# Transposing u by the DMA crossbar from SBUF to SBUF instead of by TensorE, with held x loads and zero fills on ScalarE, in a causal conv + low-rank mixer kernel

## The chip, the cores and the metric

One core of a Trainium2 chip. The metric is the device time of one execution in microseconds (us); the tables give the median of the executions. Engines are called as the profile calls them: PE is TensorE's matmul, PEld its weight load, DVE VectorE, ACT ScalarE, POOL GpSimd, SP SyncE, which only issues DMAs here; SPq is its queue.

## The reference

Inputs are float32, B = 8 batches, S = 4224 tokens, D = 192 channels in 8 heads of 24.

```python
w = softmax(weight)                                   # 8 heads x 7 taps
y[b, s, h, :] = sum_k w[h, k] * x[b, s - 6 + k, h, :] # causal conv, zeros before the start
h = (y^T @ U) @ V                                     # low rank 32, along the sequence
u = y + h^T
out = u + relu(u @ w_ch1) @ w_ch2                     # 192 -> 768 -> 192
```

(The names are shortened; the original computes the conv by unfolding and einsum.)

## The kernel before

Tokens are cut into 8 x 33 tiles of 128, and 8 tiles make a group, so there are 33 groups. For each group u must be turned around (channels onto partitions) before w1 can be multiplied. The kernel interleaves, in each iteration g: the w1 matmuls of group g, the w2 matmuls of group g-1, the conv of the next batch (when there is some left to do), `h_unit` (which makes u of group g+2) and the transposes of group g+1. Batch b+1's x is loaded into the buffer of batch b-1.

```python
def load_x(b):
    if b > 1:
        x_tiles[b], xh_tiles[b] = x_tiles[b - 2], xh_tiles[b - 2]
    nc.gpsimd.dma_start(out=x_tiles[b][:, 1 : 1 + NT, :], in_=x[b].rearrange(...))
    load_xh(b)
...
def tr_unit(g):
    def full():
        ps = [bank()[:].bitcast(BF16) for _ in range(2)]      # two PSUM banks
        uT = uTs.tile([P, 3, TOK], BF16, name="uT")
        for c in range(3):
            for i in range(Q):                                # 12 transposes of 128x128
                nc.tensor.transpose(out=ps[c // 2][...], in_=u_ring[:, r0 // 2 + i, c * P : (c + 1) * P],
                                    identity=ident[:])
        nc.vector.tensor_copy(out=uT[:, 0:2, :], in_=ps[0])
        nc.scalar.activation(out=uT[:, 2, :], in_=ps[1][:, 0:TOK], func=ACT.Copy)
    return None, full
...
for g in range(NG + 1):
    for k in range(2):
        if g < NG:
            for m in range(3):
                w1_piece(g, 3 * k + m, ...)       # 6 matmuls each, rhs = uT of group g
        units = side(2 * g + k)                   # conv heads, tt; after tt: load_x of the batch after
        if k and g + 2 < NG:
            units = [h_unit(g + 2, 0), h_unit(g + 2, 1)] + units
        ...
        run(*early)
        if g > 0:
            w2_piece(g - 1, k * 24, k * 24 + 12)  # also out = ch + u on DVE, and a store on SP
        run(*late)
        if k == 0 and g + 1 < NG:
            run(tr_unit(g + 1))
        if g > 0:
            w2_piece(g - 1, k * 24 + 12, k * 24 + 24)
```

The output tiles have 4 buffers, and each group makes 4 stores: DVE can run one group ahead of the stores, no more.

## Time and profile before

| | before |
|---|---|
| time, median of 4 executions | 410.61 us |
| span of the profiled execution | 407.7 us |
| PE busy | 92% |
| group without conv | 9.43 us |
| first w1 matmul at | 38.02 us |

The page of the kernel before, cut. Part 1 has busy time, share of the span and instruction count of each engine; part 3 the DMA queues with packets, MB, and the time of their packets as a share of 16 engines' span; part 4 the chain of work that ended last; part 6 the DMA issues with their count, size and median time from issue to landing.

```profile
PE 376.5 (92%) x3978; PEld 248.1 (61%) x3978; DVE 286.1 (70%) x514; ACT 218.0 (53%) x412; POOL 30.4 (7%) x34
...
q0 software_dynamic: 34960, 13.31, 28.1%
q1 hardware_dynamic: 40464, 30.04, 24.6%
...
PE 90%; ACT 4%; DVE 4%; DMA 1%; issue 1%; DVEq 0%
PE un L349 33%; PE ch L370 33%; PE un L255 7%; PE un L329 6%; PE un L244 5%; PE un L301 4%; PE un L275 2%; DVE U_sb L405 1%; DMA w_sb<-in_weight_dram 1%; DVE sm L160 1%; DVE u_ring L312 0%; ACT rl_476 L358 0%; DVE x_sb_162 L69 0%; ACT x_sb_
...
out_dram<-o SPq DMA_DIRECT2D x132, 192.0 KB, 2.0
```

PE is the bound: it is on 90% of the chain. The PE transposes (line 329) alone have 6% of it. Stores (the hardware queue, q1) and x loads (the software queue, q0) use the DMA engines about half the time.

The timeline of PE near the end, where no conv is left; columns are start and duration in us, then the instructions, merged into rows of one kind.

```profile
340.36 2.12 PE L349 MATMUL un<-uT,W_sb 64*128 64x512 bf16 x18
...
349.79 2.12 PE L349 MATMUL un<-uT,W_sb 64*128 64x512 bf16 x18
...
357.46 0.83 PE L329 MATMUL un<-ident,u_ring 128*128 128x128 bf16 x12
358.13 0.66 PE L370 MATMUL ch<-W_sb,rl_5345 128*128 128x192 bf16 x6
```

From one group's w1 start to the next is 349.79 - 340.36 = 9.43 us, with no gap. The 12 transposes start at 357.46 and the matmul after them at 358.13: they cost 0.67 us of PE's order (the duration shown, 0.83, includes the last one's drain, which overlaps).

The start of the kernel, timeline of all engines, cut to what the argument touches.

```profile
5.28 2.81 POOL L90 MEMSET xh_163<- 64x3264 f32 x1
...
5.56 2.56 DVE L160 TENSOR_SCALAR sm<-sm 128x8 f32<-128x8 f32 x1
8.15 0.20 DVE L162 RECIPROCAL rs<-sm 128x8 f32<-128x8 f32 x1
...
22.22 2.84 POOL L90 MEMSET xh_278<- 64x3264 f32 x1
...
22.56 4.67 DVE L405 STREAM_TRANSPOSE U_sb<-U_in 128x1024 bf16<-128x1024 bf16 x1
...
38.02 2.97 PE L349 MATMUL un<-uT,W_sb 64*128 64x512 bf16 x18
```

A DVE instruction on 128x8 takes 2.56 us while GpSimd fills a tile with zeros; its neighbour takes 0.20. The transpose of U takes 4.67 us while GpSimd runs another fill.

### The profile page before, as it was taken

How to read it: one execution, taken by the hardware profiler on the slowest of the kernel's cores; microseconds unless marked ns; L12 is line 12 of the kernel's file. 1: busy time of each engine (PE TensorE's matmuls, PEld its weight loads, DVE VectorE, ACT ScalarE, POOL GpSimd, SP SyncE). 2: the span in 40 equal slices, each digit the busy share in tenths (PEclk: the TensorE clock that was granted, in tenths of full speed). 3: DMA queues.
4: the chain of work that ended last, by engine and by line, in shares of the span. 5: the costliest groups of instructions: out<-in, count | busy, mean ns of one | idle time of the engine just before them, and what ended most of it. 6: DMA issues, size and time to landing. Idle time of an engine off the chain costs nothing.

```text
span 407.7 us, 9513 instructions
## 1 busy us (share of the span) xinstructions
PE 376.5 (92%) x3978; PEld 248.1 (61%) x3978; DVE 286.1 (70%) x514; ACT 218.0 (53%) x412; POOL 30.4 (7%) x34
## 2 busy tenths in 40 slices
PE   0747999999999999999999999999999999999996
PEld 1224457656666567656666567666666567677765
DVE  5466667776686767776686667766686677888863
ACT  2522766566546555566546555576456655544541
POOL 7072002000200002000200002000000000000000
PEclk9998999999999999999999999999999999999999
DMA  7999917922294218922294228922121221322234
GB/s 195 254 132 185 112 63 110 188 81 77 61 190 114 79 60 115 189 78 79 63 191 111 79 67 112 185 80 79 59 81 56 79 79 55 104 79 78 79 102 132
DMA packets 75466, 43.95 MB, mean 108 GB/s; under 512 B 36768, under 2 KB 75168, under 8 KB 75296
## 3 DMA queue, kind: packets, MB, share of 16 engines
q0 software_dynamic: 34960, 13.31, 28.1%
q1 hardware_dynamic: 40464, 30.04, 24.6%
q8 instruction: 31, 0.51, 0.5%
q14 instruction: 11, 0.09, 0.1%
HBM read 29.86 MB, written 25.95 MB: 137 GB/s over the span
## 4 chain that ended last, share of the span: by engine, by line
PE 90%; ACT 4%; DVE 4%; DMA 1%; issue 1%; DVEq 0%
PE un L349 33%; PE ch L370 33%; PE un L255 7%; PE un L329 6%; PE un L244 5%; PE un L301 4%; PE un L275 2%; DVE U_sb L405 1%; DMA w_sb<-in_weight_dram 1%; DVE sm L160 1%; DVE u_ring L312 0%; ACT rl_476 L358 0%; DVE x_sb_162 L69 0%; ACT x_sb_162 L67 0%; PE un L180 0%
## 5 line engine op out<-in xcount | busy, mean ns | idle before, releaser
L349 PE MATMUL un<-uT,W_sb 64*128 64x512 bf16 x1188 | 140.6, 379 | 0.0
L380 DVE TENSOR_TENSOR o<-ch,u_ring 128x384 f32<-128x384 f32 x132 | 73.2, 557 | 75.7 <-PE ch L370 74.8
L349 PEld LDWEIGHTS <-W_sb 64*128 64x128 bf16 x1188 | 53.3, 94 | 65.3 <-issue 11.0
L67 ACT ACTIVATE y_sb<-un 128x408 bf16<-128x408 f32 (+2 forms) x124 | 54.1, 501 | 31.2 <-PE un L255 30.9
L312 DVE TENSOR_TENSOR u_ring<-y_sb,un 128x384 bf16<-128x384 bf16 (+1 forms) x136 | 64.5, 537 | 3.3 <-PE un L301 0.6
L335 ACT ACTIVATE uT<-un 128x512 bf16<-128x512 bf16 x33 | 19.7, 597 | 23.6 <-PE un L329 22.7
L329 PE MATMUL un<-ident,u_ring 128*128 128x128 bf16 x396 | 28.6, 221 | 1.1 <-DVE u_ring L312 1.1
L244 PEld LDWEIGHTS <-bandp 64*128 64x128 bf16 x136 | 11.0, 99 | 26.3 <-issue 17.6
L329 PEld LDWEIGHTS <-u_ring 128*128 128x128 bf16 x396 | 24.3, 99 | 3.3 <-DVE u_ring L312 1.8
L255 PEld LDWEIGHTS <-band 128*128 128x128 bf16 x136 | 10.2, 103 | 25.5 <-issue 22.5
L244 PE MATMUL un<-x_sb_162,bandp 64*128 64x408 bf16 (+2 forms) x48 | 14.2, 372 | 10.1 <-DVE x_sb_162 L69 7.4
L334 DVE COPY uT<-un 128x1024 bf16<-128x1024 bf16 x33 | 22.5, 681 | 0.8 <-PE un L329 0.8
L301 PE MATMUL un<-tt_sb,V_sb 64*128 64x192 bf16 x264 | 21.6, 246 | 1.1 <-DVE tt_sb L287 1.1
L301 PEld LDWEIGHTS <-V_sb 64*128 64x128 bf16 x264 | 15.1, 94 | 10.9 <-issue 1.7
L255 PE MATMUL un<-x_sb_162,band 128*128 128x408 bf16 (+2 forms) x72 | 17.8, 367 | 0.0
L101 POOL DMA_DIRECT2D x_sb_277<-in_x_dram x4 | 7.3, 1814 | 114.9 <-PE un L255 114.9
L255 PE MATMUL un<-x_sb_277,band 128*128 128x408 bf16 x64 | 15.0, 340 | 0.0
L101 POOL DMA_DIRECT2D x_sb_162<-in_x_dram x3 | 5.4, 1812 | 90.5 <-PE un L255 86.7
L244 PE MATMUL un<-x_sb_277,bandp 64*128 64x408 bf16 x32 | 10.6, 331 | 1.7 <-ACT rl_1986 L358 0.2
L244 PE MATMUL un<-xh_278,bandp 64*128 64x408 bf16 x32 | 9.5, 331 | 2.3 <-ACT rl_476 L358 0.4
L69 DVE CAST y_sb<-un 128x288 bf16<-128x288 f32 (+1 forms) x12 | 5.1, 433 | 8.8 <-PE un L255 8.7
L180 PE MATMUL un<-taps,sel 112*128 112x128 bf16 x10 | 1.2, 306 | 9.3 <-DVE taps L171 9.3
(289 smaller groups left out, 621.4 us busy)
## 6 DMA issues: line engine op xcount, KB each, us to landing
out_dram<-o SPq DMA_DIRECT2D x132, 192.0 KB, 2.0
x_sb_277<-in_x_dram POOLq DMA_DIRECT2D x4, 1584.0 KB, 18.0
x_sb_162<-in_x_dram POOLq DMA_DIRECT2D x3, 1584.0 KB, 16.4
xf<-in_x_dram SPq DMA_DIRECT2D x2, 1152.0 KB, 11.2
xf<-in_x_dram SPq DMA_DIRECT2D x1, 864.0 KB, 17.0
W_sb<-in_moe_w_ch_dram POOLq DMA_DIRECT2D x3, 288.0 KB, 4.9
V_sb<-V_sb SPq DMA_DIRECT2D x3, 264.0 KB, 7.8
xh_278<-in_x_dram POOLq DMA_DIRECT2D x4, 72.0 KB, 17.4
```

The source lines that it names most:

```text
L67: nc.scalar.activation(out=out_ap, in_=in_ap, func=ACT.Copy)
L101: nc.gpsimd.dma_start(out=x_tiles[b][:, 1 : 1 + NT, :], in_=x[b].rearrange("(j p) d -> p j d", p=P))
L244: nc.tensor.matmul(out=st["ps"][i][:, 0 : (e - a) * GS], lhsT=bandp[rows, h, :], rhs=src[rows, a:e, h * GS : (h + 1) * GS], start=True, st ...
L255: nc.tensor.matmul(out=ps[:, 0 : (e - a) * GS], lhsT=band[:, h, :], rhs=x_tiles[b][:, a + 1 : e + 1, h * GS : (h + 1) * GS], start=False, ...
L301: nc.tensor.matmul(out=ps[i][:, k * D : (k + 1) * D], lhsT=V_sb[rows, j * P : (j + 1) * P], rhs=tt_tiles[b][rows, :], start=True, stop=True,)
L312: nc.vector.tensor_tensor(out=u_of(t0 + 2 * i + k, n), in0=in3(y_tiles[b][:, j : j + n, :]), in1=in3(ps[i][:, k * D : (k + n) * D].rearran ...
L329: nc.tensor.transpose(out=ps[c // 2][:, (c % 2) * TOK + i * P : (c % 2) * TOK + (i + 1) * P], in_=u_ring[:, r0 // 2 + i, c * P : (c + 1) * P],
L334: nc.vector.tensor_copy(out=uT[:, 0:2, :], in_=ps[0])
L335: nc.scalar.activation(out=uT[:, 2, :], in_=ps[1][:, 0:TOK], func=ACT.Copy)
L349: nc.tensor.matmul(out=h1[a][:], lhsT=W1_sb[rows, c, ms], rhs=uT[rows, c, :], start=c == 0, stop=c == 2,)
L370: nc.tensor.matmul(out=ch[g][:, t % 2, :], lhsT=rl_tiles[g][t % 2][:, m, (t // 2) * P :][:, 0:P], rhs=W2_sb[:, m, :], start=m == 0, stop=m ...
L380: nc.vector.tensor_tensor(out=in3(o[:]), in0=in3(ch[g][:]), in1=u_of(t0, 2), op=ALU.add)
```

## The change

Its intent: take the transposes and their PSUM banks off TensorE. A DMA with transposition reads u from SBUF and writes uT to SBUF, with nothing left for PE, DVE or ACT to do. It is issued as soon as u of group g+2 is made, in the second half of iteration g. The x load of the batch after waits until the first conv result of the current batch exists (a 1-element GpSimd copy reads it), and the zero fills go to ACT.

```diff
-    uTs = ctx.enter_context(tc.tile_pool(name="uTs", bufs=2))
+    uTs = ctx.enter_context(tc.tile_pool(name="uTs", bufs=3))
...
-        nc.gpsimd.memset(xh_tiles[b][:].rearrange("p t d -> p (t d)").bitcast(F32), 0.0)
...
     def load_x(b):
         if b > 1:
             x_tiles[b], xh_tiles[b] = x_tiles[b - 2], xh_tiles[b - 2]
+            nc.gpsimd.tensor_copy(out=seen[0:1], in_=y_tiles[b - 1][0:1, 0, 0:1])
...
+    zero = dum[0:C2].to_broadcast([C2, NTP * D // 2])
+    clear = [xh_tiles[b][:].rearrange("p t d -> p (t d)").bitcast(F32) for b in range(2)]
+    nc.scalar.activation(clear[1], zero, ACT.Copy)      # clear[0] the same, after tt_unit(0)
...
-    def tr_unit(g):                                     # 12 nc.tensor.transpose, 2 copies
+    def transpose(g):
+        r0 = (g * G) % RING
+        uT_tiles[g] = uTs.tile([P, Q, 3, P], BF16, name="uT")
+        nc.sync.dma_start_transpose(
+            out=uT_tiles[g][:].rearrange("p i c t -> p (i c) t"),
+            in_=u_ring[:, r0 // 2 : r0 // 2 + Q, :].rearrange("p i d -> p (i d)"),
+        )
...
-                    rhs=uT[rows, c, :],
+                    rhs=uT[rows, :, c, :],
...
     for g in range(2):
         run(h_unit(g, 0), h_unit(g, 1))
-        if g == 0:
-            run(tr_unit(0))
+        transpose(g)
...
             run(*early)
+            if k == 1 and g + 2 < NG:
+                transpose(g + 2)
...
             run(*late)
-            if k == 0 and g + 1 < NG:
-                run(tr_unit(g + 1))
```

More of the change, by code (lines that the diff above doesn't have):

```diff
@@ L145 @@
     dum = cst.tile([P, 1], F32, name="dum")
+    seen = cst.tile([P, 1], F32, name="seen")
     nc.vector.memset(dum[:], 0.0)
-    nc.scalar.activation(dum[:], dum[:], ACT.Exp)
+    nc.scalar.activation(seen[:], dum[:], ACT.Exp)
+    new_x(0)
+    new_x(1)
+    zero = dum[0:C2].to_broadcast([C2, NTP * D // 2])
+    clear = [xh_tiles[b][:].rearrange("p t d -> p (t d)").bitcast(F32) for b in range(2)]
+    nc.scalar.activation(clear[1], zero, ACT.Copy)
     mx = cst.tile([P, H, 1], F32, name="mx")
@@ L200 @@
     copy("dve", bandp[0:C2, :, 0:BLK], ps[3][0:C2, 0:P].rearrange("p (h t) -> p h t", t=BLK))
-    ident = cst.tile([P, P], BF16, name="ident")
-    nc.gpsimd.memset(ident[:], 0.0)
-    nc.gpsimd.affine_select(
-        out=ident[:],
-        in_=ident[:],
-        compare_op=ALU.not_equal,
-        fill=1.0,
-        base=0,
-        pattern=[[-1, P]],
-        channel_multiplier=1,
-    )
     u_ring = cst.tile([P, RING // 2, 2 * D], BF16, name="u_ring")
@@ L319, in h_unit @@
         return half, None
-    def tr_unit(g):
-        def full():
-            ps = [bank()[:].bitcast(BF16) for _ in range(2)]
-            r0 = (g * G) % RING
-            uT = uTs.tile([P, 3, TOK], BF16, name="uT")
-            uT_tiles[g] = uT
-            for c in range(3):
-                for i in range(Q):
-                    nc.tensor.transpose(
-                        out=ps[c // 2][:, (c % 2) * TOK + i * P : (c % 2) * TOK + (i + 1) * P],
-                        in_=u_ring[:, r0 // 2 + i, c * P : (c + 1) * P],
-                        identity=ident[:],
-                    )
-            nc.vector.tensor_copy(out=uT[:, 0:2, :], in_=ps[0])
-            nc.scalar.activation(out=uT[:, 2, :], in_=ps[1][:, 0:TOK], func=ACT.Copy)
-        return None, full
+    def transpose(g):
[5 more added lines that the diff above has]
+        )
     def w1_piece(g, m, engs):
@@ L391, in run @@
                 full()
-    new_x(0)
     for i, (a, e) in enumerate(CHUNKS):
@@ L408 @@
             )
-    nc.gpsimd.tensor_copy(out=dum[:], in_=xf[:, NT - 1, 0:1])
+    nc.gpsimd.tensor_copy(out=seen[:], in_=xf[:, NT - 1, 0:1])
     W1_sb = cst.tile([P, 3, M4], BF16, name="W1_sb")
@@ L416 @@
     nc.gpsimd.dma_start(out=W2_sb[:], in_=moe_w_ch2[:].rearrange("(m p) d -> p m d", p=P))
-    new_x(1)
     load_x(1)
     run(tt_unit(0))
+    nc.scalar.activation(clear[0], zero, ACT.Copy)
     for g in range(2):
         run(h_unit(g, 0), h_unit(g, 1))
-        if g == 0:
-            run(tr_unit(0))
+        transpose(g)
     work = {}
```

## The prediction

> **What bounds it now.** TensorE: the page has PE 92% busy, and the chain of waits that ended last is 90% PE. In the timeline of a stretch without conv the PE works back to back: one group of 8 token tiles takes 9.43 us (w1 starts at 340.36 and 349.79), with conv about 12. DVE (70%) and ACT (53%) are behind it. The first w1 matmul comes at 38 us.
>
> **What goes.** Twelve PE transposes per group. In the timeline they start at 357.46 and the next w2 matmul at 358.13: 0.67 us of the PE's order, 33 times; 32 stand in the dense stretch, 21.4 us. (The chain gives that line 5.7%, 23 us.) A 681 ns DVE copy and a 597 ns ACT copy per group go too, off the chain, so they earn nothing alone. The conv matmuls already read 24-column pieces, so reading uT in 128-column pieces should cost nothing.
>
> **Prologue.** GpSimd's zero fills take 2.81 and 2.84 us. While they run, a DVE op on 128x8 takes 2.56 us (its neighbours 0.2) and the U transpose 4.67 us, both on the chain; I expect 0.2 and 2.2 us. Against it, the ACT fill (estimate 3.2 us, from 1.16 us for 1152 columns) delays the exp of the taps by 1.3 us. Net about 3.5 us earlier.
>
> **What comes.** 33 crossbar transposes of 384 KB on SyncE's queue, which also issues the stores. Estimates: at the hardware queue's 300 GB/s (30 MB in 24.6% of the span) 1.3 us of all engines; as 1536 pieces of 256 bytes at that queue's 40 ns per packet, 3.9 us. The Trainium skill, "DMA: Bandwidth & Descriptors", latency and measured facts, has 261 GB/s for a transpose, 1.5 us; "VectorE: DVE Perf Modes", the three transpose paths, has 1309 ns for one 128x128 by crossbar, so 15.7 us for twelve if nothing overlaps. No trace here shows one yet. I take 3 to 6 us from issue to landing, up to 10 beside an x load. The transpose of group g+2 is issued in the second half of iteration g and needed when g+2 begins, about 11 us later: hidden. DMA engines are 28% busy without loads and near 90% in one (16 to 18 us per batch), so there is room. Only the first transpose is exposed: u to w1 took 2 us, now 4 to 6; about 3 us given back.
>
> Holding the x load back moves it within some 25 us of slack and keeps the load of batch 2 off the first transposes: worth about nothing by itself.
>
> **Sum.** 410.5 - 21.4 - 3.5 + 3 + 1 (some transposes late beside loads) = 389.6. I predict 389.5 us, 8 times in 10 between 383 and 404. Faster by over 2%: 0.87; within 2%: 0.05; slower: 0.08.
>
> **What would show it.** A group without conv at 8.76 us; PE still 90% of the chain; w1 not waiting for a DMA after the first group; transposes landing in 3 to 6 us; the 128x8 DVE op at 0.2 us; first w1 matmul at 36 to 38 us.
>
> **What would make it wrong.** A transpose that occupies DMA engines or SyncE's sequencer for over 9 us: then w1 waits for uT in every group, at 12 us or more, 420 us and over. Or stores stuck behind it, so that DVE waits for output buffers. Or only those beside x loads are late: 5 to 10 us lost. Or ACT or DVE (about 7.5 of 8.8 us) cannot follow the freed PE.

## More of the kernel before

All timed executions here were in the fast state. (The one profile-only run is a single execution, whose state is unknown.)

## The result, and the profile after

| | before | after |
|---|---|---|
| time, median of 4 executions | 410.61 us | 393.69 us (392.86 to 394.51) |
| ratio | | 0.9586, 95% interval 0.9561 to 0.9612 |
| span of the profiled execution | 407.7 us | 392.1 us |
| group without conv | 9.43 us | 8.76 us |
| first w1 matmul at | 38.02 us | 42.47 us |

A ratio is the mean time of one kernel's fast runs over that of the other's of the same rounds, so it is not quite the ratio of the medians quoted.

The page after, cut to the lines that answer those of before.

```profile
PE 354.3 (90%) x3582; PEld 226.0 (58%) x3582; DVE 264.0 (67%) x481; ACT 204.0 (52%) x381; POOL 25.1 (6%) x36
...
q1 hardware_dynamic: 92208, 43.03, 48.3%
q0 software_dynamic: 34960, 13.31, 29.0%
...
out_dram<-o SPq DMA_DIRECT2D x132, 192.0 KB, 2.6
...
uT<-u_ring SPq DMA_TRANSPOSE x33, 3.7
```

PE lost 22 us of busy time, and the hardware queue doubled its share. From the packets of q1, (92208 - 40464) / 33 = 1568 per transpose; as 384 KB are 1536 pieces of 256 bytes, that is 1536 of these and 32 more (the packet records of the trace have 50688 of 256 bytes, 27 ns each in the mean). Its share grew from 24.6% of 407.7 us to 48.3% of 392.1 us, 89 us of all 16 engines, 2.7 us for each transpose. (In this trace the chain of waits reaches back only to 296 us, so its shares are not shown; from there to the end it is PE nearly throughout.)

Timeline of PE near the end, and then the tile uT: the issue on SyncE's queue (minimum, median and maximum duration of the issue in ns), who waited, and the time from issue to landing.

```profile
340.45 2.12 PE L333 MATMUL un<-uT,W_sb 64*128 64x512 bf16 x18
...
349.21 2.12 PE L333 MATMUL un<-uT,W_sb 64*128 64x512 bf16 x18
```

```profile
L318 SPq DMA_TRANSPOSE uT<-u_ring x33: 1426/1454/2709, 37.4 to 366.4; - x33
...
  DMA uT<-u_ring: 5.5, 1
...
DMA to landing us min/median/max: 3.6/3.7/9.9
```

A group without conv takes 349.21 - 340.45 = 8.76 us, which is 0.67 less. w1 waited for a uT once in the whole run, 5.5 us at the start. Most transposes land in 3.7 us, the slowest in 9.9.

The start, timeline.

```profile
6.36 0.17 DVE L166 TENSOR_SCALAR sm<-sm 128x8 f32<-128x8 f32 x1
...
12.00 1.16 ACT L67 ACTIVATE x_sb_121<-xf 128x1152 bf16<-128x1152 f32 x1 [2.81 <-DMA xf<-in_x_dram]
...
23.61 4.65 DVE L388 STREAM_TRANSPOSE U_sb<-U_in 128x1024 bf16<-128x1024 bf16 x1
...
37.44 14.16 SPq L318 DMA_TRANSPOSE uT<-u_ring  x3
...
42.47 5.54 PE L333 MATMUL un<-uT,W_sb 64*128 64x512 bf16 x36 [5.45 <-DMA uT<-u_ring]
```

The DVE instruction on 128x8 is back at 0.17 us, but the transpose of U still takes 4.65 us, and the x piece was waited for until 12.00 us. The first transpose was issued at 37.44 and released w1 at 42.47, 5.03 us later. By PE, u's last piece was written at 36.28 and w1 began at 38.02, 1.7 us later.

The two profiled spans differ by 15.6 us. From the first w1 to that of the last group 21.1 us were won (each group after the first is 0.67 us shorter; 32 x 0.67 = 21.4), the start gave back 42.47 - 38.02 = 4.45 us, and the end another 1.0. The medians of all executions differ by 16.9 us.

### The profile page after: what moved, and what is told of

It reads as the page before. It is cut to its first block, busy times and chain, and to the rows that moved or that the text cites. A ratio compares the mean times of both kernels' runs of the same rounds, so it can differ in the third digit from the quotient of the medians.

```text
span 392.1 us, 8704 instructions
## 1 busy us (share of the span) xinstructions
PE 354.3 (90%) x3582; PEld 226.0 (58%) x3582; DVE 264.0 (67%) x481; ACT 204.0 (52%) x381; POOL 25.1 (6%) x36
## 3 DMA queue, kind: packets, MB, share of 16 engines
q1 hardware_dynamic: 92208, 43.03, 48.3%
## 5 line engine op out<-in xcount | busy, mean ns | idle before, releaser
L100 POOL CAST seen<-y_sb 1x1 f32<-1x1 bf16 x6 | 1.1, 178 | 210.9 <-ACT y_sb L67 210.9
L238 PE MATMUL un<-x_sb_125,bandp 64*128 64x408 bf16 x32 | 10.6, 331 | 1.7 <-ACT rl_445 L342 0.2
L238 PE MATMUL un<-xh_126,bandp 64*128 64x408 bf16 x32 | 9.5, 331 | 2.3 <-ACT rl_444 L342 0.4
L281 DVE TENSOR_TENSOR tt_sb<-un,sw 128x192 bf16<-128x192 f32 x8 | 2.9, 358 | 8.7 <-ACT sw L279 8.7
L238 PE MATMUL un<-xh_122,bandp 64*128 64x408 bf16 x24 | 7.1, 330 | 1.8 <-ACT rl_1152 L342 0.2
L269 PE MATMUL un<-y_sb,U_sb 128*32 128x192 bf16 x264 | 8.0, 262 | 0.0
L342 ACT ACTIVATE rl_355<-un 128x512 bf16<-128x512 f32 x6 | 3.6, 597 | 7.6 <-PE un L333 7.4
L101 POOL DMA_DIRECT2D x_sb_125<-in_x_dram x4 | 7.3, 1821 | 1.4 <-PE ch L354 1.4
```

The lines of the kernel that those rows point to most:

```text
L238: nc.tensor.matmul(out=st["ps"][i][:, 0 : (e - a) * GS], lhsT=bandp[rows, h, :], rhs=src[rows, a:e, h * GS : (h + 1) * GS], start=True, st ...
L269: nc.tensor.matmul(out=ps[q * R : (q + 1) * R, 0:D], lhsT=U_sb[:, j, :], rhs=y_tiles[b][:, j, :], start=j < 4, stop=j >= NT - 4,)
L342: nc.scalar.activation(out=rl[a][:, m, :], in_=h1[a][:], func=ACT.Relu)
```

## The experiments

All twelve runs computed correct results. Ratios are to the kernel before, timed on the same chip in the same rounds; it took 410.34 us (runs of 1 to 4), 410.66 (5 to 8) and 410.52 (9 to 12).

| run | what | us | ratio, 95% interval |
|---|---|---|---|
| pe_kept | fills and hold only, PE transposes kept | 408.86 | 0.9965, 0.9951 to 0.9980 |
| pe_first | after, group 0 transposed on PE | 387.51 | 0.9442, 0.9427 to 0.9457 |
| no_hold | after, x loads not held | 412.77 | 1.0051, 1.0017 to 1.0085 |
| gp_fills | after, fills on GpSimd | 393.51 | 0.9591, 0.9569 to 0.9612 |
| after_again | after, unchanged | 392.34 | 0.9556, 0.9539 to 0.9574 |
| u_late_pe_first | pe_first, U transposed later | 384.82 | 0.9371, 0.9351 to 0.9392 |
| ghost | after, and idle PE transposes | 414.64 | 1.0097, 1.0078 to 1.0117 |
| late_issue | after, crossbar issued later | 443.66 | 1.0789, 1.0758 to 1.0820 |
| no_hold_out8 | no_hold, 8 output buffers | 404.28 | 0.9855, 0.9829 to 0.9881 |
| hold_first | hold for batch 2 only | 405.44 | 0.9878, 0.9855 to 0.9902 |
| no_hold_act | no_hold, stores from ACT's queue | 434.05 | 1.0587, 1.0554 to 1.0620 |
| u_twice | after, a second U transpose | 395.4 (one look) | |

### Is it PE's order that was won? (ghost, pe_kept)

ghost does the PE transposes at their old place as well, with no copies out:

```diff
+    ident = ...                                   # as in the kernel before
+    def ghost(g):                                 # tr_unit without its two copies
+        ...
             run(*late)
+            if k == 0 and g + 1 < NG:
+                run(ghost(g + 1))
```

> The changed kernel, with the 12 TensorE transposes per group done as well, at their old place, into two PSUM banks that nothing reads: no copies out. Theory (the gain is TensorE's own order; the copies out were off the chain): 32 x 0.67 us come back, 413 to 416 us, groups without conv at 9.43 us. Rival (the copies on VectorE and ScalarE were part of the gain): clearly less comes back, 403 to 410 us.

Measured 414.64 us, beside 392.34 for the unchanged after in the same rounds: 22.3 us came back, where 32 x 0.67 = 21.4 were expected. It still has no copies out, so those were not part of the gain. Its timeline has the transposes 9.43 us apart again:

```profile
352.09 0.83 PE L333 MATMUL un<-ident,u_ring 128*128 128x128 bf16 x12
...
361.52 0.83 PE L333 MATMUL un<-ident,u_ring 128*128 128x128 bf16 x12
```

pe_kept has the other parts of the change without the crossbar:

```diff
-        transpose(g)            # and transpose(g + 2) in the loop
+        if g == 0:
+            run(tr_unit(0))     # and run(tr_unit(g + 1)) in the loop, as before
```

> The zero fills on ScalarE and the held loads as in the changed kernel, but the transposes still on TensorE. Theory (the gain is the 0.67 us per group that TensorE no longer spends): no gain here, ratio to the kernel before between 0.995 and 1.003, groups without conv at 9.43 us. Rival (the fills and the hold carry part of the gain): 2 us or more faster, ratio 0.995 or below.

Measured 0.9965: 1.5 us faster. The band of the first theory reached down to 0.995, so this lies in it, but the gain is clear of noise: the fills and the hold together are worth 1.5 us in a kernel without the crossbar. In its trace w1 begins at 37.07 instead of 38.02 us and a group without conv still takes 9.43, so what shows there is at the start.

### What is the hold on the x loads worth? (no_hold, no_hold_out8, hold_first)

```diff
-            nc.gpsimd.tensor_copy(out=seen[0:1], in_=y_tiles[b - 1][0:1, 0, 0:1])
```

> As the changed kernel, without the hold on the x loads. Theory (the loads have slack, and so do all transposes but the first; the first meets the load of batch 1 in any case): within 1 us of the changed kernel, 393 to 395 us, no more waits of w1 for uT. Rival (the hold keeps the crossbar's transposes in time): 396 us or more, with w1 waiting for uT in groups 1 to 3 and after each batch.

Measured 412.77 us: without the hold the whole gain is gone, and 2 us more. The rival was right, and the prediction's sentence that the hold is "worth about nothing by itself" was wrong by about 20 us. Who waited for whom, in no_hold (engine and line, whom it waited for, total us, times, longest):

```profile
DVE o L363 <- DMA out_dram<-o: 23.6, 11, 4.6
PE un L332 <- DMA uT<-u_ring: 16.4, 6, 11.6
```

Transposes and stores in flight beside an x load, first in no_hold and then in after (count, size, median us to landing of those issued in a short stretch):

```profile
out_dram<-o SPq DMA_DIRECT2D x4, 192.0 KB, 9.5
uT<-u_ring SPq DMA_TRANSPOSE x1, 10.6
```

```profile
out_dram<-o SPq DMA_DIRECT2D x4, 192.0 KB, 6.7
uT<-u_ring SPq DMA_TRANSPOSE x1, 9.5
```

These two transposes landed in 10.6 and 9.5 us; alone one takes 3.7. When it must be there differs too. Timeline of both, x loads on POOL, transposes on SPq, w1 on PE:

```profile
71.73 1.81 POOL L100 DMA_DIRECT2D x_sb<-in_x_dram  x1 [34.77 <-PE un L248]
...
78.65 3.11 SPq L317 DMA_TRANSPOSE uT<-u_ring  x1
...
78.91 2.12 PE L332 MATMUL un<-uT,W_sb 64*128 64x512 bf16 x18
...
89.28 2.12 PE L332 MATMUL un<-uT,W_sb 64*128 64x512 bf16 x18 [0.19 <-DMA uT<-u_ring]
```

```profile
82.22 1.45 SPq L318 DMA_TRANSPOSE uT<-u_ring  x1
...
83.05 1.82 POOL L101 DMA_DIRECT2D x_sb_125<-in_x_dram  x1 [0.37 <-PE ch L354]
...
93.54 2.56 SPq L318 DMA_TRANSPOSE uT<-u_ring  x1
...
95.23 2.12 PE L333 MATMUL un<-uT,W_sb 64*128 64x512 bf16 x18
...
106.55 2.12 PE L333 MATMUL un<-uT,W_sb 64*128 64x512 bf16 x18
```

Without the hold the load starts at 71.73, when the conv of a batch has just been finished, so it lies beside the groups with the least conv. There a transpose's lead, from its issue to the w1 that needs it, is 10.4 us (73.53 to 83.91 in after). The transpose issued at 78.65 lands after 10.6 us, at 89.24, and w1 begins at 89.28. With the hold the load starts at 83.05, just behind a transpose that still lands in 3.7 us, and beside groups with more conv: the transpose issued at 93.54 takes 9.5 us, and is not needed before 106.55, 13 us later.

This one transpose put w1 back by only 0.3 us. What the whole run lost is read from the starts of w1, group by group, against a second profile of the unchanged after (after_again, below). In no_hold the transposes that met the five later loads landed in 10.6 to 12.2 us and put w1 back by 0.3 to 1.8 us each, 5.1 in all. The group after each of them was 1.3 to 2.1 us longer, 8.2 in all, and there DVE waited for stores. The start, up to the w1 of the third group, took 6.6 us more. Together these are 19.9 of the 20.2 us between the two spans (410.3 and 390.1). So the hold moves the load from where 10.4 us of lead are just too few to where 13 are enough, but at the later loads the late transposes cost less than the late stores.

Why "no_hold" also stalls DVE: the stores stand behind the transpose in the same queue, took 9.5 us there, and only 4 output buffers exist. DVE's longest wait for a store beside this load:

```profile
90.52 0.56 DVE L363 TENSOR_TENSOR o<-ch,u_ring 128x384 f32<-128x384 f32 x1 [3.21 <-DMA out_dram<-o]
```

Eight buffers test it:

```diff
-    outs = ctx.enter_context(tc.tile_pool(name="outs", bufs=4))    # in no_hold
+    outs = ctx.enter_context(tc.tile_pool(name="outs", bufs=8))
```

> Without the hold, and with 8 output buffers in place of 4. The run without the hold lost 11.4 us of TensorE's time after the start: 6.6 us in waits behind VectorE, which waited for stores, and 4.8 us for uT. Theory (late stores and late transposes each carry their part): VectorE's waits for stores go, 6 us come back, 405 to 408 us. Rival A (it is all the stores): 11 us or more come back, 402 us or less. Rival B (late transposes set the pace and the buffers only moved the wait): 411 us or more, the waits for uT growing to 10 us.

Measured 404.28 us, 8.5 us back by the medians and 6.6 by the profiled spans; 6 were expected. The five groups after a late transpose are as long as in after again, so the 8.2 us there were the stores; 2.0 us of them went into transposes that now came 7.1 us late instead of 5.1. The wait of DVE for stores fell from 23.6 us to 2.2, and PE's for uT grew a little:

```profile
PE un L332 <- DMA uT<-u_ring: 18.7, 6, 12.0
...
DVE o L363 <- DMA out_dram<-o: 2.2, 5, 0.4
```

Last, the hold for one load only:

```diff
-            nc.gpsimd.tensor_copy(out=seen[0:1], in_=y_tiles[b - 1][0:1, 0, 0:1])
+            if b == 2:
+                nc.gpsimd.tensor_copy(out=seen[0:1], in_=y_tiles[b - 1][0:1, 0, 0:1])
```

> Hold only for the load of batch 2, which without it is queued behind the load of batch 1 just ahead of the first transposes. Theory (that load costs about 6.5 us at the start, 11.6 against 5.1 us of wait, and the loads of batches 3 to 7 the rest): 403 to 406 us. Rival (all of it is the start): 393 to 395 us.

Measured 405.44 us, as the theory said, and 7.3 us less than no_hold by the medians. In the profiles 5.1 us of that are the start, where the load of batch 2 is queued ahead of the first transposes (w1 began at 47.12 us in no_hold and at 42.00 here). The other 12 to 13 us come from the five later loads, about 2.5 us each: the groups at these loads are 12.2 us longer than in after_again.

### The stores from another queue (no_hold_act)

```diff
-                nc.sync.dma_start(out=out_t[:, t0 : t0 + 2, :], in_=o[:])    # in no_hold
+                nc.scalar.dma_start(out=out_t[:, t0 : t0 + 2, :], in_=o[:])
```

> Without the hold, and the stores issued from ScalarE's queue instead of SyncE's. Theory (stores beside a load are late since they stand behind a transpose in the same queue; in a queue of their own they share the engines in turn): stores land in 4 to 6 us even beside a load, VectorE's waits for them go, some 5 us back, 406 to 409 us. Rival (the DMA engines themselves are the limit): stores still take 9 us beside a load, no gain.

A miss for both theories: 434.05 us. DVE's waits for stores did fall (to 5.5 us), and the stores that met the second load landed in 7.3 us at the median, but the transposes beside a load now took up to 16.4 us. The chain of waits of this kernel, in order of time (start, us, what), has five pieces of 14.5 to 16.5 us in which a transpose is on its way beside a load; one of them, with the w1 matmuls after it:

```profile
78.25 16.07 DMA uT<-u_ring
94.36 3.80 PE un L332 x18
```

The Trainium skill, "DMA: Bandwidth & Descriptors", section "Queues, rings and completion order", says that each DMA engine serves the queues that have work in turn, packet by packet. The numbers fit that: a transpose lands in 3.7 us alone, in 10.6 to 12.2 beside the load's queue in no_hold (13.0 at most, at its start with two loads queued), and in 14.5 to 16.5 with a third queue at work; the median of all transposes rose from 3.8 to 5.1 us. Read so, the stores' own queue took a share from the transpose, and the transpose was the one that PE waited for. Group by group against after_again, the late transposes put w1 back by 25.7 us here and by 5.1 in no_hold. The groups after them were 7.5 us longer, since w1's first 18 matmuls take 3.3 to 4.0 us after the wait instead of 2.12; in no_hold the late stores made these groups 8.2 us longer. The differences, 25.7 - 5.1 and 7.5 - 8.2, sum to 19.9 us, of 20.0 between the two spans (430.3 and 410.3). What no run separates is whether the two hardware queues hinder each other in some other way too, and what the 0.38 us per store that ACT now spends on issuing adds.

### How early must the transpose be issued? (late_issue)

```diff
-            if k == 1 and g + 2 < NG:
-                transpose(g + 2)
...
             run(*late)
+            if k == 0 and g + 1 < NG:
+                transpose(g + 1)
```

> The changed kernel, with each crossbar transpose issued where the TensorE transposes stood: in the group before it is needed, some 5 us ahead instead of 9 to 11. Theory (landing takes 3.7 us alone and 9 to 10 us beside an x load): no waits for uT away from loads, 2 to 5 us for each transpose that meets a load (two of them in each of 6 loads), so 415 us, between 405 and 425. Rival (the lead is more than needed even beside loads): within 2 us of the changed kernel.

Measured 443.66 us. The theory's kind was right, its size was not: 51 us were lost, where 23 were expected and 32 was the most. Away from loads there were indeed no waits but the last group's 0.3 us (the median landing is 3.7 us here too). In all PE waited 41.8 us for uT in 8 waits:

```profile
PE un L333 <- DMA uT<-u_ring: 41.8, 8, 6.7
```

One of these waits, timeline of PE:

```profile
203.38 2.14 PE L354 MATMUL ch<-W_sb,rl 128*128 128x192 bf16 x24
210.84 4.02 PE L333 MATMUL un<-uT,W_sb 64*128 64x512 bf16 x18 [5.33 <-DMA uT<-u_ring]
```

After the wait the 18 w1 matmuls took 4.02 us where they take 2.12 otherwise, so a wait costs more than itself. Of the 41.8 us, 5.9 are the wait at the start, which the unchanged after has too (5.1 to 5.5), and 0.3 are in the last group. The other six waits, one for each later load, are 36 us, and the groups that begin with them are about 2.3 us longer each, 14 in all, 1.9 us of each in those 18 matmuls. That is 50 of the 51. The theory had expected two late transposes for each load, of 2 to 5 us; it was one, of 5.2 to 6.7, and the expectation had left the slow matmuls out.

### The start (pe_first, after_again)

```diff
     for g in range(2):
         run(h_unit(g, 0), h_unit(g, 1))
-        transpose(g)
+        if g == 0:
+            run(tr_unit(0))       # on PE, as before; ident is built again
+        else:
+            transpose(g)
```

> As the changed kernel, but the transposes of group 0 alone on TensorE. Theory (the start gives back some 3.3 us because the first crossbar transpose is exposed, and 0.9 us more because TensorE's first matmuls after that wait are slow): 389 to 391 us, about 3 to 4 us less than the changed kernel; first w1 matmul at about 39 us, its first 18 matmuls in about 3 us. Rival (the later start comes from the x load landing later, not from the transpose): no change, 393 to 394 us.

> The changed kernel once more, for comparison on one chip with the runs beside it, and to see whether the first piece of x lands at 12 us again. Theory (its landing at 12 us was that one execution): 393 to 394 us, the piece landing at 9.5 to 10.5 us as in four later runs. Rival (the changed kernel itself delays it): 12 us again.

Measured 387.51 us for pe_first, lower than expected, and 392.34 for after again. The piece of x that landed at 12.00 us in the first profile of after was used from 9.64 us in the second, and between 9.5 and 11.1 in all the others: that delay belongs to the one execution, not to the change. The second profile is then the fair one to compare with pe_first. Timelines, the first w1 matmuls of each, after_again first:

```profile
39.67 6.87 PE L333 MATMUL un<-uT,W_sb 64*128 64x512 bf16 x36 [5.06 <-DMA uT<-u_ring]
```

```profile
37.10 5.04 PE L367 MATMUL un<-uT,W_sb 64*128 64x512 bf16 x36
```

w1 begins 2.6 us earlier, and its first 36 matmuls take 5.04 us instead of 6.87. The sum, 4.4 us, is the difference of the two spans (390.1 and 385.7). So the exposed first crossbar transpose costs 2.6 us of later start and 1.8 us of slow matmuls after PE's 5.06 us of idling. The Trainium skill, "TensorE: Matmul & The Clock Gate", section "What's actually happening", has PE at half its clock after an idle stretch of about 3.4 us. The traces agree in effect: w1's matmuls are up to 1.9 times as long after a wait of about 5 us (late_issue, where the granted clock was 0.50 in the 4 us after three of these waits), and the mean granted clock between 37 and 48 us was 0.62 in after_again and 1.00 in pe_first. But the first profile of after had slow matmuls too (36 in 5.54 us, where two runs of 18 take 2.05 + 2.12 = 4.17) at a recorded clock of 1.00 between 40 and 50 us, so the record does not always show it; in no_hold_act the 18 after a wait of only 2.47 us took 3.80; and no run here tested the clock by itself.

### The zero fills and the U transpose (gp_fills, u_twice, u_late_pe_first)

```diff
-    nc.scalar.activation(clear[1], zero, ACT.Copy)     # and clear[0]
+    nc.gpsimd.memset(clear[0], 0.0)                    # and clear[1], before load_x(1)
```

> As the changed kernel, with the zero fills back on GpSimd. Theory (taking them off shortened the DVE op on 128x8, but the time is lost again waiting for x to land): within 1 us of the changed kernel, the DVE op at about 2.5 us again, the U transpose at 4.6 to 4.7 us as in both kernels. Rival (the fills off GpSimd are worth their 1.6 us of earlier taps, or more): 395.5 us or more.

Measured 393.51 us, no different from after. The DVE instruction took 2.08 us again, ending with the fill, but ACT did not wait for x then; in the runs with the fills on ACT it waited 0.4 to 2.8 us for it, so the short instruction won little. The Trainium skill, "SBUF — State Buffer", section "Who interferes with whom", has GpSimd and some DVE instructions share one pair of ports, held for a whole instruction; the 2.56 and 2.08 us beside a fill, and 0.17 without, agree. The U transpose was as long as ever, which u_twice settles with a second one at a time when GpSimd does nothing:

```diff
+            if g == 3 and k == 0:
+                nc.vector.transpose(out=spare[:].rearrange("p j r -> p r j"), in_=U_in[:].rearrange("p i r -> p r i"))
```

> The changed kernel with a second U transpose into a spare tile in group 3, when GpSimd neither fills nor issues anything. Theory (4.65 us is the op itself): 4.6 to 4.7 us again. Rival (GpSimd's DMA issues stretch it at the start): 2 to 3 us.

```profile
74.17 4.67 DVE L442 STREAM_TRANSPOSE spare<-U_in 128x1024 bf16<-128x1024 bf16 x1
```

It takes 4.67 us by itself; GpSimd had nothing to do with it. So the useful thing is to take it off the chain. In u_late_pe_first it comes after the cast of the last piece of x rather than before it, and that piece's conv copies are all on ACT, with group 0 transposed on PE:

```diff
-        if i == 1:
-            nc.vector.transpose(out=U_sb[:, 0:NU, :]..., in_=U_in...)      # at the end of piece 1
+        if i == 2:
+            nc.vector.transpose(out=U_sb[:, 0:NU, :]..., in_=U_in...)      # after the casts of piece 2
+        eng = ("act", "act") if i == 2 else ("act", "dve")
```

> Group 0 transposed on TensorE, and the U transpose on VectorE moved behind the cast of the last piece of x, with that piece's conv copies all on ScalarE. Theory (the U transpose takes 4.65 us of VectorE by itself, GpSimd or not, and was on the chain at the start): it still takes 4.6 to 4.7 us, the first w1 matmul about 3 us earlier, 384 to 385 us. Rival (ScalarE's eight copies take as long as what is saved): no gain over 387.5 us.

Measured 384.82 us, 0.9371 of before: the fastest of all, faster than both kernels, and by the ratios 2.9 us below pe_first. (The run moved the U transpose and the copies together, so what each gave is not separated.) w1 begins at 34.92 us here, though x landed 1.1 us later than in pe_first's profile.

## Why the prediction was right or wrong

The time was right: 389.5 us was predicted, 383 to 404 as the range, and 393.69 measured. By its points:

- **PE's order, 21.4 us.** Right. A group without conv went from 9.43 to 8.76 us, and ghost put 22.3 us back. That the copies out were worth nothing alone is shown by the same run.
- **Cost of a crossbar transpose, 3 to 6 us, up to 10 beside an x load.** Right for the kernel as changed: 3.7, and 8.3 to 9.9 beside a load. The packet count confirms the 256-byte pieces, but that they gave 3.9 us was partly luck: the 40 ns per packet came from the stores, whose packets have 768 bytes. A 256-byte packet took 27 ns, which makes 2.7 us over the 16 engines; the other 1.0 us to landing is not in the packets' time. Twelve times the skill's 1309 ns was four times too much.
- **Lead of about 11 us, "hidden".** Right with the hold: in after_again the leads run from 8.6 to 13.3 us, and every transpose but the first landed at least 3.1 us before it was needed. Without the hold it does not stand: 10.4 us of lead beside a load, against a landing of 10.6 to 12.2.
- **"Worth about nothing by itself"**, of the hold. This is the step that failed. It is worth 1.5 us at most without the crossbar (pe_kept, fills included), but about 20 us with it (no_hold, 412.77 against 392.34 to 393.69). The prediction counted the load's own slack, some 25 us, and did not ask what the load does to the DMAs beside it at one time and at the other: 6.6 us at the start, 5.1 in late transposes and 8.2 in late stores. It named late transposes and stuck stores as things that would make it wrong, but did not tie them to the hold. That the time came out right is luck in this point: the line that it valued at nothing was in the kernel, and without it the time is 412.77 us, outside 383 to 404.
- **Stores behind the transpose.** It was named as a thing that would make the prediction wrong. It happens only without the hold, and 8 buffers then give 8.5 us back by the medians.
- **The start: 3.5 us won, 3 lost, and w1 at 36 to 38 us.** Wrong in its terms. Of the win, the 128x8 instruction came true (2.56 to 0.17 us) and mostly vanished in waiting for x, and the U transpose did not change (4.65 us, where 2.2 were expected), since its length is its own. The loss was 3.3 us for the first transpose (5.03 against 1.7) and more for slow matmuls after the wait, which the prediction left out. Where 0.5 us were to be won in all, the net was a w1 that began 1.7 us (second profile) to 4.45 us (first) later than before. pe_first got it back.

What is left open: what made x land late in the first profile of after, whether the slow matmuls after a wait are the clock gate, which was not tested by itself, and whether the sharing between queues is the whole cause of no_hold_act's loss.

## What to carry to other kernels

Here TensorE worked back to back, and taking work out of its order paid that work's time. The DMA that replaces it is free only if it is issued earlier than its landing time under the worst traffic, not the median one; 3.7 us alone became 8 to 12 beside a load, and 16 beside a load and a third queue. What stands behind it in its queue, here the stores, comes late with it. So place a bulk load where the groups are long and just after a transpose has been issued, rather than as soon as its buffer is free. At the start, where nothing hides the first transfer, keep the short path: one group on TensorE was worth about 5 us.

## What the Trainium skill lacked or had wrong

- "VectorE: DVE Perf Modes", "The three transpose paths", gives the crossbar 1309 ns for a 128x128 block, and does not say how the time grows with the number of blocks. Twelve blocks in one DMA land in 3.7 us here, 0.31 us for each, so the figure must not be multiplied.
- "DMA: Bandwidth & Descriptors", "Latency and other measured facts", gives 261 GB/s for a DMA transpose with a non-contiguous middle dimension, and 350 to 400 for the contiguous case. From issue to landing, 393 KB in 3.7 us are 106 GB/s; by queue time (2.7 us) they are 146. The page has a 256-byte tile for the transpose ("SDMA does more than copy"), but not what one costs: here 1536 packets of 256 bytes for each transpose, 27 ns each.
- The same page, "Rules for kernel authors", has "A transpose next to ordinary DMAs needs nothing". The row is about corruption, and all runs were correct. Of time the page says nothing: 3.7 us became 8.3 to 12.2 beside an x load, and up to 16.4 with the stores on a third queue.
- The same page, "Issuing engines are not separate DMA queues", says that issuing from several engines only saves issue time. Here moving the stores to another queue (no_hold_act) made the kernel 21 us slower than no_hold, with transposes beside a later load landing in 14.5 to 16.5 us instead of 10.6 to 12.2. The page's own section on queues lets one expect a changed share; this sentence does not.
- "VectorE: DVE Perf Modes" gives DVE 311 ns for 128x128 in 32x32 blocks, which would be 2.5 us for 128x1024 (an estimate from it). With an input and an output that both step 64 bytes from element to element it took 4.65 to 4.67 us in every run; whether the steps are the reason was not tested.
